# Decode block with adaLN, cached attention and a SiLU feed-forward: a smaller first transfer, and 16 value rows scaled on another engine

## The chip, the core and the metric

The kernel runs on one core of a Trainium2 chip. A core has TensorE (PE: matmuls), VectorE (DVE), ScalarE (ACT), GpSimd (POOL) and SyncE (SP), which here issues all DMAs; 16 DMA engines carry them out. The metric is the device time of one execution in microseconds (us), the median of several runs. Lower is better.

## The reference

Everything is float32. There are 4 batches, each with one token of width 512, 32 heads with 4096 cached keys and values of width 128, and a feed-forward part of width 1792.

```python
mod = (_silu(c) @ w_mod).reshape(4, 6, 1, -1)
sa, ca, ga, sb, cb, gb = (mod[:, i] for i in range(6))
h = _layernorm(x) * (1 + ca) + sa
q = (h @ wq).reshape(B, 1, H, Dh).transpose(0, 2, 1, 3)
scores = einsum("bhqd,bhkd->bhqk", q, k_cache) * Dh ** -0.5
o = einsum("bhqk,bhkd->bhqd", softmax(scores), v_cache)
x = x + ga * (o as (B, 1, H * Dh)) @ wo
h = _layernorm(x) * (1 + cb) + sb
return x + gb * (silu(h @ w1) @ w2)
```

The key and value caches are 4 x 32 x 4096 x 128 floats each, 268 MB each; they are read once. All else together is about 30 MB.

## The kernel before, in words

**Slots.** SBUF holds three slots of 64 KB per partition (`kv`, three buffers). Everything large goes through them in order: the head (`wm`: the conditioning `c`, the input `x` and the modulation weights `w_mod`), `wq`, then for each of 32 iterations n one K tile and one V tile, at the end `wo` and the two feed-forward weights. A K or V tile is 128 partitions x 128 rows x 128 floats: one batch and four heads, 32 partitions for each head. SyncE issues a transfer when its slot is free. K of the next iteration is issued at an iteration's start, V after the K reductions (`load_k`, `load_v`).

**The start.** One transfer (L118) brings the head on 128 partitions, 12320 floats each: four rows of `w_mod` per partition with 16 floats of `c` and 16 of `x` in front. Meanwhile VectorE and GpSimd build constants. When it has landed, `silu2` makes `csT`, `mods((sa, ca1), 0)` multiplies it with the weights in four steps (L200), spreads the result with a VectorE product and a small matmul for each of four groups (L208, L212; the products alternate between two halves of `mm`), then comes the layernorm, then `mods` for the other four vectors, then the query product with `wq` (L249). Small tiles of this stage lie in the head's own slot behind the weights: `mm`, `qs`, `zsel`, `csT`, `hT` and others. K1 and V0 take the slots of the head and of `wq`.

**An iteration n of the main loop.** The K tile is multiplied with the query, 104 of its 128 rows by VectorE and 24 by GpSimd (L283; the first two iterations divide it otherwise), then VectorE adds over the width (L288). Then comes a chain of small steps: row maximum (L292, VectorE), a transpose on TensorE (L296), maximum per head on VectorE (L301 to L304), exponential on ScalarE (L310), spread weights on GpSimd (L316, `pz`).

The V tile of iteration n - 1 is weighted in three ways. Rows 64 to 127 go through TensorE with the spread weights (`pv`, L356). Rows 0 to 47 are multiplied on GpSimd (L331). Rows 48 to 63 are multiplied on ScalarE, 16 activations with a scale for each partition (L330). Then GpSimd adds the 64 multiplied rows in halves, 32, 16, 8, 4 (L335), and TensorE adds the remaining four groups into the sum (`vsum`, L341), which frees V's slot. The last two V tiles go through TensorE whole.

At certain iterations finished heads are gathered and normalized (`gather`, `norm`, `spread`). After the loop come the output product, the second layernorm and the feed-forward part, whose last weights arrive in small pieces (L477 with `fetch`).

Of the kernel before, what the change touches and what calls it, by code (L numbers as in the profile page):

```python
# [9 lines left out]
F32 = mybir.dt.float32  # L10
# [7 lines left out]
def kernel(  # L18
    ctx: ExitStack,
    tc: tile.TileContext,  # L20
    head: bass.AP,
    kc: bass.AP,
    vc: bass.AP,
# [12 lines left out]
    HP = 4  # L36
# [12 lines left out]
    NK = D // P  # L49
    NI = F // P  # L50
    FG = F // G
    NA = 24
    NL = 56
    NV = 64
# [45 lines left out]
        load(vt, vc, "v", n)  # L100

    s0 = Slot("wm")
    cT, xT = s0.take(NK, B), s0.take(NK, B)
    wmt = s0.take(NK, 6 * D)
    nh = s0.at
    hg0, sa, ca1 = (s0.take(P) for _ in range(3))
    tmp = s0.take(NK, B)
    mm = s0.take(2, 4, P)
    csT, hT, xw = (s0.take(NK, W) for _ in range(3))
    CW = HP * Dh  # L110
    qs = s0.take(2, CW)
    ZB = P - NT * B // 2
    zsel = s0.take(ZB + P)

    xg = const.tile([P, P], F32, name="xg")
    nc.vector.memset(csT, 0.0)
    nc.gpsimd.memset(xw, 0.0)
    nc.sync.dma_start(s0.t[:, :nh], head)  # L118
    wqt = Slot("wq").take(NK, H * Dh)
    nc.sync.dma_start(wqt, wq.rearrange("p (k n) -> p k n", k=NK))  # L120
    load_k(0, 0, NJ // 2, NJ)
# [57 lines left out]
    nc.vector.memset(zsel, 0.0)  # L179
    nc.vector.tensor_copy(zsel[:, ZB:P].rearrange("p (g x) -> p g x", g=G), i4[:, :, ::SB])  # L180

    def silu2(dst, t, src):
        nc.scalar.activation(t, src, AF.Tanh, scale=0.5)
        nc.vector.scalar_tensor_tensor(dst, t, 1.0, src, op0=ALU.add, op1=ALU.mult)  # L184
# [10 lines left out]
    def mods(dsts, i):  # L195
        n = len(dsts)
        p = psum([P, D], "q", 2)
        for k in range(NK):
            for u in range(n):
                nc.tensor.matmul(  # L200
                    p[W * u : W * (u + 1), :], csT[:, k, :], wmt[:, k, (i + u) * D : (i + u + 1) * D],
                    start=k == 0, stop=k == NK - 1,
                )
        z = psum([P, n, P], "q", 2)
        r = W * n
        for g in range(G):
            m = mm[:r, g % 2, :n, :]
            nc.vector.tensor_mul(  # L208
                m, p[:r, g * P : (g + 1) * P].unsqueeze(1).to_broadcast([r, n, P]),
                hm[:r, :n].unsqueeze(2).to_broadcast([r, n, P]),  # L210
            )
            nc.tensor.matmul(z[W * g : W * (g + 1), :, :], sel[:r, :], m, start=True, stop=True)  # L212
        for u, d in enumerate(dsts):
            nc.scalar.activation(
                d, z[:, u, :], AF.Copy,
                scale=0.25 if i + u == 5 else 0.5, bias=1.0 if i + u in (1, 4) else 0.0,
            )
# [59 lines left out]
        qw[n] = work.tile([P, Dh], F32, tag="qw", name=f"qw{n}")  # L277
        nc.scalar.activation(qw[n], qb[n], AF.Copy)  # L278

    sc, nm, po, rs = {}, {}, {}, {}  # L280

    def mult(eng, src, n, lo, hi):
        eng.tensor_mul(  # L283
# [8 lines left out]
        nc.vector.tensor_reduce(nm[n], sc[n], axis=AX.X, op=ALU.max)  # L292

    def bmax(n):
        p = psum([P, P + HP], "mx", 2)
        nc.tensor.transpose(p[:, :P], nm[n].to_broadcast([P, P]), ident)  # L296
        nm[n] = p

    def negmax(n):
        m = nm[n][:, P:]  # L300
        nc.vector.tensor_reduce(m, nm[n][:, :P].rearrange("p (i x) -> p i x", i=HP), axis=AX.X, op=ALU.max)  # L301
# [24 lines left out]
    def vmult(n):  # L326
        if first(n):
            v = vt[n]
            for j in range(NP, NV):
                nc.scalar.activation(v[:, j, :], v[:, j, :], AF.Copy, scale=sc[n][:, j : j + 1])  # L330
            nc.gpsimd.tensor_mul(  # L331
                v[:, :NP, :], v[:, :NP, :], sc[n][:, :NP].unsqueeze(2).to_broadcast([P, NP, Dh])
            )
            for m, lo in ((32, 32), (16, 16), (8, 8), (JJ, JJ)):
                nc.gpsimd.tensor_add(v[:, :m, :], v[:, :m, :], v[:, lo : lo + m, :])  # L335
# [111 lines left out]
    for n in range(N):  # L447
        t, b = divmod(n, B)
        if n + 1 < N:
            load_k(n + 1)  # L450
        else:
            load_v(n)
        if t and b == 1:
            sums(t - 1)
        sc[n] = work.tile([P, NJ], F32, tag="sc", name=f"sc{n}")
        w, m = (NJ // 2, NL // 2) if n == 0 else (NJ, NL) if n == 1 else (NJ, NA)
        for lo in range(0, NJ, w):
            mult(nc.gpsimd, qw, n, lo, lo + m)
            mult(nc.vector, qb, n, lo + m, lo + w)
            if n + 1 < N and not lo:  # L460
                make_qb(n + 1)
            if n:
                vmult(n - 1)
                pv(n - 1)
            red(n, lo + m, lo + w)
        for lo in range(0, NJ, w):
            red(n, lo, lo + m)
        if n + 1 < N:
            load_v(n)
        else:  # L470
            so = Slot("wo")
            wat, wot = so.take(RA, D), so.take(NT - TA, R, D)
            fetch(so.t, wo, 0, RA * D, SLOT - R * D, SLOT)
            s2 = Slot("w12")
            w1t = s2.take(NK, F)
            w2t = s2.take(NI, D)
            fetch(s2.t, w12, 0, 3 * F, *(NK * F + i * D for i in (0, 5, 8, 10, 11, 12, 13, 14)))  # L477
        rowmax(n)
        bmax(n)
        if n and first(n - 1):  # L480
            vsum(n - 1)
        negmax(n)
# [69 lines left out]
def _packed(inputs):  # L552
# [39 lines left out]
```

## Time and profile before

| | before |
|---|---|
| median of 3 runs | 1319.3 us (1318.99 to 1319.37) |
| profiled execution, span from the first to the last instruction | 1317.4 us (the profile states no other time of this execution) |
| mean granted TensorE clock | 0.597 |
| VectorE busy | 1077.5 us, 82% |
| GpSimd busy | 1074.5 us, 82% |
| TensorE, ScalarE busy | 338.3 us, 196.0 us |
| DMA queue fed by SyncE | 567.31 MB, 99.5% of 16 engines' span |

How to read it: the busy share of an engine is an average over stages. The DMA share is the time in which a packet was under way, over 16 engines. In rows of instructions the columns are start, duration, engine, line, operation, output<-inputs, and in brackets the idle time before with what ended it; in grouped rows they are busy time, mean duration in ns, and idle time before with its releasers. Times are in us from the span's start.

### The profile page before, as it was taken

The numbers are of one execution on the slowest core, as the hardware profiler recorded it, in microseconds if no ns is written. First come the engines' busy times: TensorE is split into PE (matmuls) and PEld (weight loads), VectorE is DVE, ScalarE is ACT, GpSimd is POOL, SyncE is SP. The second block draws the span as 40 slices with busy tenths as digits, with TensorE's granted clock in tenths as the row PEclk, the third lists the DMA queues.
The fourth block names the chain that finished last, engine by engine and source line by source line (L and its number), as shares of the span: only waits on it lengthen the run. The fifth ranks groups of instructions, "written<-read, shape, count | busy, mean of one in ns | idle before, by whom it ended". The sixth has DMA issues, their size and how long they took to land.

```text
span 1317.4 us, 5041 instructions
## 1 busy us (share of the span) xinstructions
PE 338.3 (26%) x1636; PEld 88.8 (7%) x1636; DVE 1077.5 (82%) x357; ACT 196.0 (15%) x648; POOL 1074.5 (82%) x227
## 2 busy tenths in 40 slices
PE   3301122221212222121322122122212223221258
PEld 1100000000000000000000000000000000000013
DVE  2597888988888998888898888889888889988862
ACT  1101111110111111012111111111201121110101
POOL 0459888888988888998888899888889888889910
PEclk9756656655665565556655555655655665655569
DMA  9999999999999999999999999999999999999998
GB/s 414 436 422 444 434 428 440 424 440 440 423 440 440 426 438 434 430 437 436 432 438 428 432 440 432 432 440 430 430 442 430 432 434 436 434 434 430 440 422 342
DMA packets 11434, 567.63 MB, mean 431 GB/s; under 512 B 1280, under 2 KB 1296, under 8 KB 2192
## 3 DMA queue, kind: packets, MB, share of 16 engines
q1 hardware_dynamic: 11408, 567.31, 99.5%
q8 instruction: 13, 0.21, 0.1%
q14 instruction: 13, 0.11, 0.0%
HBM read 567.30 MB, written 0.01 MB: 431 GB/s over the span
## 4 chain that ended last, share of the span: by engine, by line
DMA 48%; DVE 28%; POOL 21%; PE 2%; issue 1%; ACT 0%; SPq 0%; DVEq 0%; POOLq 0%
DMA k<-in_A_k_cache_dram 21%; DMA v<-in_A_v_cache_dram 20%; DVE sc L288 16%; POOL v L335 13%; DVE k L283 12%; POOL v L331 8%; DMA w<-in_B_w_dram 3%; DMA wq<-in_A_wq_dram 3%; PE po L341 1%; PE q L249 1%; PE mx L259 0%; ACT qm L272 0%; PE q L274 0%; SPq L86 0%; PE od L378 0%
## 5 line engine op out<-in xcount | busy, mean ns | idle before, releaser
L283 DVE TENSOR_TENSOR k<-k,q 128x13312 f32<-128x13312 f32 (+2 forms) x33 | 440.3, 13343 | 151.2 <-DMA k<-in_A_k_cache_dram 136.4
L288 DVE TENSOR_REDUCE sc<-k 128x104 f32<-128x13312 f32 (+3 forms) x66 | 553.2, 8423 | 4.1
L335 POOL TENSOR_TENSOR v<-v 128x4096 f32<-128x4096 f32 (+1 forms) x120 | 508.9, 4241 | 9.4
L331 POOL TENSOR_TENSOR v<-v,sc 128x6144 f32<-128x6144 f32 x30 | 313.8, 10461 | 109.9 <-DMA v<-in_A_v_cache_dram 109.9
L356 PE MATMUL po<-v,pz 128*32 128x512 f32 x1088 | 193.3, 876 | 270.0 <-DMA v<-in_A_v_cache_dram 270.0
L283 POOL TENSOR_TENSOR k<-k,qw 128x3072 f32<-128x3072 f32 (+2 forms) x33 | 231.5, 7016 | 32.2 <-ACT qw L278 31.4
L341 PE MATMUL po<-v,hs 128*32 128x512 f32 x60 | 57.4, 1060 | 447.7 <-POOL v L335 447.7
L330 ACT ACTIVATE v<-v,sc 128x128 f32<-128x128 f32 x480 | 143.7, 388 | 162.8 <-DMA v<-in_A_v_cache_dram 162.8
L278 ACT ACTIVATE qw<-q 128x128 f32<-128x128 f32 x32 | 8.9, 278 | 532.8 <-DVE k L283 424.1
L356 PEld LDWEIGHTS po<-v,pz 128*32 128x32 f32 x1088 | 48.9, 153 | 417.4 <-issue 417.4
L296 PE MATMUL mx<-ident,rm 128*128 128x128 f32 x32 | 14.2, 444 | 229.6 <-DVE rm L292 229.6
L310 ACT ACTIVATE sc<-sc,nm 128x128 f32<-128x128 f32 x32 | 12.9, 402 | 328.6 <-DVE nm L304 328.6
L316 POOL TENSOR_TENSOR pz<-sc,hm 128x256 f32<-128x256 f32 x34 | 20.8, 613 | 30.6 <-ACT sc L310 30.6
L341 PEld LDWEIGHTS po<-v,hs 128*32 128x32 f32 x60 | 5.5, 140 | 456.4 <-POOL v L335 456.4
L301 DVE TENSOR_REDUCE mx<-mx 128x4 f32<-128x128 f32 x32 | 9.6, 300 | 19.4 <-PE mx L296 19.4
L296 PEld LDWEIGHTS mx<-ident,rm 128*128 128x128 f32 x32 | 5.7, 179 | 259.5 <-issue 204.9
L367 DVE TENSOR_TENSOR o<-po,jm 128x512 f32<-128x512 f32 x16 | 10.9, 681 | 12.1 <-PE po L356 12.1
L373 DVE TENSOR_REDUCE s<-o 128x128 f32<-128x512 f32 x16 | 16.6, 1036 | 0.6
L274 PE MATMUL q<-qm,blk 128*128 128x512 f32 x16 | 15.3, 1055 | 1.7 <-ACT qm L272 1.7
L200 PE MATMUL q<-wm 128*32 128x512 f32 x48 | 9.2, 681 | 18.9 <-DVE wm L184 18.9
L190 POOL COPY wm<-wm 128x16 f32<-128x16 f32 x1 | 0.2, 212 | 16.1 <-DMA wm<-in_head_dram 16.1
L272 ACT ACTIVATE qm<-qn,sel 128x128 f32<-128x128 f32 x32 | 10.2, 390 | 5.0 <-DVE oa L420 4.9
(114 smaller groups left out, 165.9 us busy)
## 6 DMA issues: line engine op xcount, KB each, us to landing
k<-in_A_k_cache_dram SPq DMA_DIRECT2D x2, 4096.0 KB, 51.8
wm<-in_head_dram SPq DMA_DIRECT2D x1, 6160.0 KB, 17.7
wo<-in_A_wo_dram SPq DMA_DIRECT2D x1, 4096.0 KB, 16.7
wo<-in_A_wo_dram SPq DMA_DIRECT2D x1, 3072.0 KB, 23.6
w<-in_B_w_dram SPq DMA_DIRECT2D x1, 2688.0 KB, 31.4
w<-in_B_w_dram SPq DMA_DIRECT2D x1, 1280.0 KB, 35.7
wo<-in_A_wo_dram SPq DMA_DIRECT2D x1, 1024.0 KB, 25.6
w<-in_B_w_dram SPq DMA_DIRECT2D x4, 256.0 KB, 17.5
```

What stands on the lines that cost most here:

```text
L249: nc.tensor.matmul(pq[i][W * g : W * (g + 1), :], hT[:, k, :], wqt[:, k, ch * CW : (ch + 1) * CW], start=k == 0, stop=k == NK - 1,)
L274: nc.tensor.matmul(p, blk.rearrange("p i x -> p (i x)"), m, start=True, stop=True)
L283: eng.tensor_mul(kt[n][:, lo:hi, :], kt[n][:, lo:hi, :], src[n].unsqueeze(1).to_broadcast([P, hi - lo, Dh]))
L288: nc.vector.tensor_reduce(sc[n][:, lo:hi], kt[n][:, lo:hi, :], axis=AX.X, op=ALU.add)
L296: nc.tensor.transpose(p[:, :P], nm[n].to_broadcast([P, P]), ident)
L316: nc.gpsimd.tensor_mul(pz[h][:, f * W : HG * W].rearrange("p (g x) -> p g x", g=m)[:, :, E:].rearrange("p g (i j) -> p g i j", i=HP), sc[n ...
L330: nc.scalar.activation(v[:, j, :], v[:, j, :], AF.Copy, scale=sc[n][:, j : j + 1])
L331: nc.gpsimd.tensor_mul(v[:, :NP, :], v[:, :NP, :], sc[n][:, :NP].unsqueeze(2).to_broadcast([P, NP, Dh]))
L335: nc.gpsimd.tensor_add(v[:, :m, :], v[:, :m, :], v[:, lo : lo + m, :])
L341: nc.tensor.matmul(po[t, q][0:W, :], hs[:, o : o + W], vt[n][:, :JJ, :].rearrange("p j d -> p (j d)"), start=False, stop=a == 1,)
L356: nc.tensor.matmul(po[t, q][W * g : W * (g + 1), :], pz[h][:, o : o + W], vt[n][:, JJ * j : JJ * (j + 1), :].rearrange("p j d -> p (j d)") ...
L373: nc.vector.tensor_reduce(s, o.rearrange("p j d -> p d j"), axis=AX.X, op=ALU.add)
```

## The change

Two things are changed.

*The head.* `w_mod` has 512 rows. The first 128 of them now come by themselves, two rows each on partitions 32 to 95 (`first_rows`). The other 384, three per partition on 128 partitions, come in a second transfer, with `c` and `x` now behind them. The modulation product thus has five steps instead of four: in the first two only 64 partitions carry weights, and the others are set to zero on VectorE and GpSimd (32 partitions each) beforehand; `c` is laid out to match. `mm` (now one buffer instead of two), `qs` and `zsel` move to memory of their own, outside of the head's slot.

*The value rows 48 to 63.* ScalarE's 16 activations are gone. ScalarE copies the 16 weights of each partition into PSUM behind the maxima (`wv`), and VectorE multiplies all 16 rows in one instruction of 128x2048 (`vrest`), in the next iteration, after its row maximum. GpSimd's adds are put in another order: rows 24 to 47 onto 0 to 23, 16 to 23 onto 0 to 7, then (`vadd`, with VectorE's result) 48 to 63 onto 0 to 15, then 8 and 4. Besides, two pieces of the last feed-forward weights come as one.

The core of the diff:

```diff
+    NH = 2
+    NM = NK - NH // 2
+    PH = slice(P // 4, 3 * P // 4)
...
+    half = wmt[:, :NH, :]
+    nc.sync.dma_start(s0.t[PH, : NH * 6 * D], first_rows)
+    nc.sync.dma_start(s0.t[:, NH * 6 * D : nh + (NH + NM + NK) * B], head)
     nc.vector.memset(csT, 0.0)
     nc.gpsimd.memset(xw, 0.0)
-    nc.sync.dma_start(s0.t[:, :nh], head)
...
+    nc.vector.memset(half[: PH.start], 0.0)
+    nc.gpsimd.memset(half[PH.stop :], 0.0)
...
-        for k in range(NK):
+        for k in range(NH + NM):
...
-            m = mm[:r, g % 2, :n, :]
+            m = mm[:r, :n, :]
...
+        if first(n):
+            nc.scalar.activation(wv[n], sc[n][:, NP:NV], AF.Copy)
...
-            for j in range(NP, NV):
-                nc.scalar.activation(v[:, j, :], v[:, j, :], AF.Copy, scale=sc[n][:, j : j + 1])
...
-            for m, lo in ((32, 32), (16, 16), (8, 8), (JJ, JJ)):
-                nc.gpsimd.tensor_add(v[:, :m, :], v[:, :m, :], v[:, lo : lo + m, :])
+            fold(n, (24, 24), (8, 16))
+
+    def fold(n, *steps):
+        v = vt[n]
+        for m, lo in steps:
+            nc.gpsimd.tensor_add(v[:, :m, :], v[:, :m, :], v[:, lo : lo + m, :])
+
+    def vadd(n):
+        if first(n):
+            fold(n, (16, NP), (8, 8), (JJ, JJ))
+
+    def vrest(n):
+        if first(n):
+            v = vt[n][:, NP:NV, :]
+            nc.vector.tensor_mul(v, v, wv[n].unsqueeze(2).to_broadcast([P, NV - NP, Dh]))
...
         rowmax(n)
+        if n:
+            vrest(n - 1)
+            vadd(n - 1)
         bmax(n)
```

How instructions move on three engines. SyncE at the program's start, before (shapes are partitions x floats):

```order
L118 DMA wm_69<-in_head_dram 128x12320
L120 DMA wq_74<-in_A_wq_dram 128x16384
L86 DMA k0_76<-in_A_k_cache_dram 128x8192 x2
L86 DMA k1_266<-in_A_k_cache_dram 128x16384
L86 DMA v0_279<-in_A_v_cache_dram 128x16384
```

And SyncE at the same place after:

```order
L122 DMA wm_69<-in_first_dram 64x6144
L123 DMA wm_69<-in_head_dram 128x9252
L127 DMA wq_78<-in_A_wq_dram 128x16384
L90 DMA k0_80<-in_A_k_cache_dram 128x8192 x2
L90 DMA k1_278<-in_A_k_cache_dram 128x16384
L90 DMA v0_291<-in_A_v_cache_dram 128x16384
```

One transfer has become two; what follows keeps its order.

VectorE at the end of iteration 3 before, from the last K reduction (`sc` are the scores, `rm` the row maximum, `mx` the PSUM tile with the transposed maxima):

```order
L288 TENSOR_REDUCE sc3_413<-k3_352 128x24
L292 TENSOR_REDUCE rm3_467<-sc3_413 128x1
L301 TENSOR_REDUCE mx_469<-mx_469 128x4
L302 TENSOR_TENSOR mx_469<-mx_469,hn_98 128x4
L304 TENSOR_REDUCE nm3_474<-mx_469 128x1
```

And VectorE at the same place after:

```order
L298 TENSOR_REDUCE sc3_400<-k3_352 128x24
L302 TENSOR_REDUCE rm3_436<-sc3_400 128x1
L359 TENSOR_TENSOR v2_380<-v2_380,mx_388 128x2048
L312 TENSOR_REDUCE mx_442<-mx_442 128x4
L313 TENSOR_TENSOR mx_442<-mx_442,hn_102 128x4
L315 TENSOR_REDUCE nm3_447<-mx_442 128x1
```

The multiply of the previous iteration's V tile has come between the row maximum and the maximum per head.

GpSimd with the V tile of iteration 1 before, up to the spread weights of iteration 2:

```order
L331 TENSOR_TENSOR v1_339<-v1_339,sc1_294 128x6144
L335 TENSOR_TENSOR v1_339<-v1_339 128x4096
L335 TENSOR_TENSOR v1_339<-v1_339 128x2048
L335 TENSOR_TENSOR v1_339<-v1_339 128x1024
L335 TENSOR_TENSOR v1_339<-v1_339 128x512
L316 TENSOR_TENSOR pz1_114<-sc2_354,hm_96 128x16x16
```

And GpSimd at the same place after:

```order
L342 TENSOR_TENSOR v1_334<-v1_334,sc1_307 128x6144
L350 TENSOR_TENSOR v1_334<-v1_334 128x3072
L350 TENSOR_TENSOR v1_334<-v1_334 128x1024
L350 TENSOR_TENSOR v1_334<-v1_334 128x2048
L350 TENSOR_TENSOR v1_334<-v1_334 128x1024
L350 TENSOR_TENSOR v1_334<-v1_334 128x512
L329 TENSOR_TENSOR pz1_118<-sc2_354,hm_100 128x16x16
```

The first add has become two smaller ones that need GpSimd's own rows alone; the add of 2048, the third now, is the first to need the rows of another engine.

More of the change, by code (lines that the diff above doesn't have):

```diff
@@ L20 @@
     tc: tile.TileContext,
+    first_rows: bass.AP,
     head: bass.AP,
@@ L102 @@
     s0 = Slot("wm")
-    cT, xT = s0.take(NK, B), s0.take(NK, B)
-    wmt = s0.take(NK, 6 * D)
+    wmt = s0.take(NH + NM, 6 * D)
     nh = s0.at
+    cT, xT = s0.take(NH + NM, B), s0.take(NK, B)
     hg0, sa, ca1 = (s0.take(P) for _ in range(3))
-    tmp = s0.take(NK, B)
-    mm = s0.take(2, 4, P)
-    csT, hT, xw = (s0.take(NK, W) for _ in range(3))
+    tmp = s0.take(NH + NM, B)
+    mm = const.tile([P, 4, P], F32, name="mm")
+    csT = s0.take(NH + NM, W)
+    hT, xw = (s0.take(NK, W) for _ in range(2))
     CW = HP * Dh
-    qs = s0.take(2, CW)
+    qs = const.tile([P, 2, CW], F32, name="qs")
     ZB = P - NT * B // 2
-    zsel = s0.take(ZB + P)
+    zsel = const.tile([P, ZB + P], F32, name="zsel")
     xg = const.tile([P, P], F32, name="xg")
+    half = wmt[:, :NH, :]
+    nc.sync.dma_start(s0.t[PH, : NH * 6 * D], first_rows)
+    nc.sync.dma_start(s0.t[:, NH * 6 * D : nh + (NH + NM + NK) * B], head)
     nc.vector.memset(csT, 0.0)
     nc.gpsimd.memset(xw, 0.0)
-    nc.sync.dma_start(s0.t[:, :nh], head)
     wqt = Slot("wq").take(NK, H * Dh)
@@ L201, in mods @@
                     p[W * u : W * (u + 1), :], csT[:, k, :], wmt[:, k, (i + u) * D : (i + u + 1) * D],
-                    start=k == 0, stop=k == NK - 1,
+                    start=k == 0, stop=k == NH + NM - 1,
                 )
@@ L278, in make_qb @@
         nc.scalar.activation(qw[n], qb[n], AF.Copy)
-    sc, nm, po, rs = {}, {}, {}, {}
+    sc, nm, po, rs, wv = {}, {}, {}, {}, {}
     def mult(eng, src, n, lo, hi):
@@ L294, in bmax @@
     def bmax(n):
-        p = psum([P, P + HP], "mx", 2)
+        p = psum([P, P + HP + NV - NP], "mx", 2)
         nc.tensor.transpose(p[:, :P], nm[n].to_broadcast([P, P]), ident)
@@ L299, in negmax @@
     def negmax(n):
-        m = nm[n][:, P:]
+        m = nm[n][:, P : P + HP]
+        wv[n] = nm[n][:, P + HP :]
         nc.vector.tensor_reduce(m, nm[n][:, :P].rearrange("p (i x) -> p i x", i=HP), axis=AX.X, op=ALU.max)
@@ L476 @@
             w2t = s2.take(NI, D)
-            fetch(s2.t, w12, 0, 3 * F, *(NK * F + i * D for i in (0, 5, 8, 10, 11, 12, 13, 14)))
+            fetch(s2.t, w12, 0, 3 * F, *(NK * F + i * D for i in (0, 5, 10, 11, 12, 13, 14)))
         rowmax(n)
+        if n:
+            vrest(n - 1)
+            vadd(n - 1)
         bmax(n)
@@ L560, in columns @@
         return a.reshape(-1, dm).T.reshape(p, -1)
+    rows, n = i["w_mod"], 2 * (p // 2)
+    c = np.zeros((p, 5, i["c"].shape[0]), i["c"].dtype)
+    c[p // 4 : 3 * p // 4, :2] = i["c"][:, :n].T.reshape(p // 2, 2, -1)
+    c[:, 2:] = i["c"][:, n:].T.reshape(p, 3, -1)
     late = i["A_wo"][half:].reshape(4, p, -1).transpose(1, 0, 2).reshape(p, -1)
     return {
-        "head": np.concatenate([columns(i["c"]), columns(i["A_x"]), i["w_mod"].reshape(p, -1)], axis=1),
+        "first": rows[:n].reshape(p // 2, -1),
+        "head": np.concatenate([rows[n:].reshape(p, -1), c.reshape(p, -1), columns(i["A_x"])], axis=1),
         "A_k_cache": i["A_k_cache"],
```

## The prediction

> **What bounds the kernel now.** I read the first page of the profile first: the engines' shares, the DMA rows, the queues.
>
> ```profile
> span 1317.4 us, 5041 instructions
> PE 338.3 (26%) x1636; PEld 88.8 (7%) x1636; DVE 1077.5 (82%) x357; ACT 196.0 (15%) x648; POOL 1074.5 (82%) x227
> DMA  9999999999999999999999999999999999999998
> DMA packets 11434, 567.63 MB, mean 431 GB/s; under 512 B 1280, under 2 KB 1296, under 8 KB 2192
> q1 hardware_dynamic: 11408, 567.31, 99.5%
> q8 instruction: 13, 0.21, 0.1%
> q14 instruction: 13, 0.11, 0.0%
> ```
>
> VectorE and GpSimd are busy for 82% each, but the queue that SyncE feeds keeps the 16 DMA engines busy for 99.5% of the span. Next the busy times by stage, from 0 to 40 us, 120 to 1040 us and the last 47 us (length, then PE, PEld, DVE, ACT, POOL busy, clock, DMA share, GB/s).
>
> ```profile
> 0.00:40.00 40.00, 16.99 (x88) 4.58 (x92) 11.27 (x47) 4.28 (x10) 2.01 (x10) 1.00 0.96 408
> 120.00:1040.00 920.00, 213.14 (x886) 50.68 (x886) 797.52 (x213) 146.84 (x497) 823.32 (x168) 0.57 1.00 434
> 1270.00:1317.40 47.40, 36.89 (x315) 13.78 (x315) 10.60 (x28) 4.67 (x9) 1.18 (x2) 0.88 0.86 363
> ```
>
> In the long middle the share is 1.00 at 434 GB/s: nothing is to be had there except by moving fewer bytes, and the change moves the same ones. What is not at that rate is the start, (434 - 408) x 40 / 434 = 2.4 us, and the end. So a faster compute engine gains nothing by itself, and a slower one costs something only if it lets the queue run dry. How far it is from that I read from the DMA issues (median us from issue to landing; KB each where all are alike).
>
> ```profile
> wm<-in_head_dram SPq DMA_DIRECT2D x1, 6160.0 KB, 17.7
> v<-in_A_v_cache_dram SPq DMA_DIRECT2D x32, 26.4
> k<-in_A_k_cache_dram SPq DMA_DIRECT2D x31, 28.1
> out_dram<-end SPq DMA_DIRECT2D x1, 8.0 KB, 1.8
> ```
>
> The head met an empty queue: 6160 KB is 6.31 MB, 14.5 us at 434 GB/s, so an idle start costs 17.7 - 14.5 = 3.2 us. One K or V transfer is 128 x 16384 x 4 B = 8.39 MB, 19.3 us. A V transfer therefore stands behind other bytes for 26.4 - 19.3 = 7.1 us, and could be issued 7.1 - 3.2 = 3.9 us later before an engine idles; a K transfer 28.1 - 19.3 - 3.2 = 5.6 us later. These two leads are the yardstick for every compute cost below.
>
> **VectorE gets 30 instructions.** The rows by form (busy, mean ns, idle before), and then VectorE in the iterations that begin near 1045 and 1084 us.
>
> ```profile
> L283 DVE TENSOR_TENSOR k<-k,q 128x13312 f32<-128x13312 f32 x30 | 420.6, 14022 | 136.4 <-DMA k<-in_A_k_cache_dram 136.4
> L367 DVE TENSOR_TENSOR o<-po,jm 128x512 f32<-128x512 f32 x16 | 10.9, 681 | 12.1 <-PE po L356 12.1
> 1044.80 14.02 DVE L283 TENSOR_TENSOR k<-k,q 128x13312 f32<-128x13312 f32 x1 [3.38 <-DMA k<-in_A_k_cache_dram]
> 1076.27 0.29 DVE L292 TENSOR_REDUCE rm<-sc 128x1 f32<-128x128 f32 x1
> 1077.18 0.30 DVE L301 TENSOR_REDUCE mx<-mx 128x4 f32<-128x128 f32 x1 [0.63 <-PE mx L296]
> 1084.12 14.02 DVE L283 TENSOR_TENSOR k<-k,q 128x13312 f32<-128x13312 f32 x1 [5.64 <-DMA k<-in_A_k_cache_dram]
> ```
>
> The new multiply of 128x2048 does not occur before. By the large product it takes 14022 x 2048 / 13312 = 2.16 us, by the small one at most 4 x 681 = 2.72 us; I take 2.2, since it is one long instruction like the first. It stands after the row maximum, where VectorE idles 0.63 us for TensorE's transpose, and that wait now runs beside it; so an iteration gains about 1.6 us of VectorE work. Behind it in the queue come the three small steps of the maximum, the exponential on ScalarE that waits for them, the gathers, and the next K product. But that product waits for K's DMA anyway: 136.4 us over 30, 4.5 us each, 3.4 us in the iteration with a gather. With 2.2 us more, and in such iterations the transpose also behind the multiply, 1.2 us of that is left. And the V transfer that follows a K reduction is released by the last reduce, ahead of the new instruction. Cost: nothing; if the cover were gone, the first 3.9 us of lateness would still lie in the lead. GpSimd's last 16-tile add now waits for this multiply. The multiply would have ended at 1076.27 + 0.29 + 2.2 = 1078.8.
>
> ```profile
> 1064.11 10.46 POOL L331 TENSOR_TENSOR v<-v,sc 128x6144 f32<-128x6144 f32 x1 [3.65 <-DMA v<-in_A_v_cache_dram]
> L335 POOL TENSOR_TENSOR v<-v 128x4096 f32<-128x4096 f32 x30 | 264.4, 8813 | 2.3
> L335 POOL TENSOR_TENSOR v<-v 128x1024 f32<-128x1024 f32 x30 | 70.6, 2354 | 2.4
> ```
>
> GpSimd reaches that add after its 10.46 us product, a 24-tile and an 8-tile add. 1024 elements cost (8813 - 2354) / 3 = 2.15 us, so 24 tiles cost 8.81 - 2.15 = 6.66 us: 1064.11 + 10.46 + 6.66 + 2.35 = 1083.6, 4.8 us after the multiply ends. No wait. The add chain is 6.66 + 2.35 instead of 8.81 ahead of the same last three adds: 0.2 us longer, plus one gap, say 0.3 us, out of a K lead of 5.6 and of 3.65 us idle. Cost: nothing. ScalarE loses 480 activations and gains 30 small ones; nobody waits for it now but the exponential.
>
> **Fewer instructions to fetch.** The two instruction queues share the DMA engines. One fetch each, from a 5 us stretch at 41 us and a 2 us stretch at 82 us (packets, MB, share of 16 engines):
>
> ```profile
> q8 instruction: 1, 0.02, 1.2%
> q14 instruction: 1, 0.01, 1.0%
> ```
>
> One 16 KB fetch holds one engine 0.012 x 16 x 5 = 0.96 us, one of 8 KB 0.010 x 16 x 2 = 0.32 us. All fetches are 0.32 MB for 5041 instructions, 63.5 B each. The 450 fewer on ScalarE are 28.6 KB, some 85 more on VectorE, GpSimd and TensorE 5.4 KB: three 8 KB fetches fewer. They help only where they sat on the engine that finishes last. The DMA row in 40 slices from 1306 to 1314 us shows that the engines don't finish together:
>
> ```profile
> DMA  9898989799899999989687867654443261210000
> ```
>
> They drop out one by one from about 1309 to 1313.4. Gain between 0 and 3 x 0.32 = 0.9 us; the larger 0.96 us fetches, which TensorE's 3272 instructions explain (0.21 MB), weigh more and stay. I take 0.1.
>
> **The start.** The bytes are the same, in 64 descriptors of 24 KB and then 128 of 37 KB instead of 128 of 49 KB. What shorter first descriptors can save is part of the 3.2 us: not more than 3.2 - 1.8 = 1.4 us, by the 16-row transfer at the end, which took 1.8 us in all; at worst nothing, since the later transfer stands in the queue before the first is done (an issue takes 0.33 us, as K3's row below shows; the first transfer's 1.57 MB take 3.6 us). I take 0.4, nearer to the old head, which it resembles more. That 64 rows still use 16 engines I read from the packets: 1280 of under 512 B are 16 for each of the 80 DMA issues, so even the 16-row output marked all 16.
>
> Here a rule speaks against the change. The Trainium skill, "SBUF — State Buffer", section "Door 1: The DMA port swizzle", says that partitions 0 to 63 reach only 8 of 16 ports and run at half rate; by its formula 32 to 95, used here, reach all 16. No trace so far shows a 64-partition load; if its half rate applied, the sum would be the rival below, if its formula does, my sum stands.
>
> The two memsets of 32x6144 are new ahead of the activations:
>
> ```profile
> 5.35 0.26 DVE L179 MEMSET wm<- 128x240 f32 x1
> 18.48 0.21 POOL L190 COPY wm<-wm 128x16 f32<-128x16 f32 x1 [16.08 <-DMA wm<-in_head_dram]
> ```
>
> At 0.26 us / 240 = 1.08 ns an element they take at most 6.7 us each, GpSimd's inside 16.08 us of waiting for the head; VectorE, idle until the same transfer lands and ScalarE's activation after it, has its own list done at 5.6 us. Nothing. (If GpSimd were twice as slow, 13.4 us would still fit.) The modulation then gets longer: five steps instead of four, and one product buffer instead of two.
>
> ```profile
> 18.94 5.52 PE L200 MATMUL q<-wm 128*32 128x512 f32 x16 [18.94 <-DVE wm L184]
> 24.51 0.75 DVE L208 TENSOR_TENSOR wm<-q,hm 64x256 f32<-64x256 f32 x2 [5.32 <-PE q L200]
> 25.63 0.75 DVE L208 TENSOR_TENSOR wm<-q,hm 64x256 f32<-64x256 f32 x2 [0.38 <-PE q L212]
> 28.17 3.64 PE L200 MATMUL q<-wm 128*32 128x512 f32 x32
> 31.88 1.29 DVE L208 TENSOR_TENSOR wm<-q,hm 128x512 f32<-128x512 f32 x2 [1.74 <-PE q L200]
> 33.77 1.29 DVE L208 TENSOR_TENSOR wm<-q,hm 128x512 f32<-128x512 f32 x2 [0.61 <-PE q L212]
> 36.20 0.79 ACT L214 ACTIVATE mod<-q 128x128 f32<-128x128 f32 x4 [7.10 <-PE q L212]
> 37.88 7.07 PE L249 MATMUL q<-wq,wm 128*32 128x512 f32 x64 [1.71 <-DMA wq<-in_A_wq_dram]
> ```
>
> A fifth step: a quarter of 5.52 and of 3.64, 1.4 + 0.9 us. One buffer: a product waits for the matmul of the one before, so each takes the distance that now holds two, 1.12 and 1.89 us: two such distances more each time, 2.2 + 3.8 us at most. That is 5 to 8.3 us on 36.99 (the last ACT row's end), against the weights that land at 37.9: the query product ends 4 to 7 us later than 44.95. I take 5.5. Behind it stand K1's load and the first products of GpSimd and VectorE, so the first transfers that feel it are V1 (issued 106.54) and K3 (127.07). The chain's V1 row, GpSimd's V0 wait, K3's issue and its landing:
>
> ```profile
> 106.54 29.23 DMA v<-in_A_v_cache_dram
> 97.31 10.46 POOL L331 TENSOR_TENSOR v<-v,sc 128x6144 f32<-128x6144 f32 x1 [1.70 <-DMA v<-in_A_v_cache_dram]
> 127.07 0.33 SPq L86 DMA_DIRECT2D k<-in_A_k_cache_dram  x1
> 155.14 14.02 DVE L283 TENSOR_TENSOR k<-k,q 128x13312 f32<-128x13312 f32 x1 [5.50 <-DMA k<-in_A_k_cache_dram]
> ```
>
> V1's lead is 29.23 - 19.3 - 3.2 = 6.7 us, K3's 28.07 - 22.5 = 5.6, of which 5.5 - 1.7 + 0.3 = 4.1 is used. Both hold, by 1.2 and 1.5 us; at the upper end V1 falls 0.3 us short. After that VectorE waits for the DMA again and the delay is gone.
>
> **The sum.** Start -0.4, fetches -0.1, the rest hidden: -0.5 us on a span of 1317.4. The median of the runs, 1319.3, lies 1.9 us above the span (the profile gives no other time of its execution); I keep that difference: 1318.8.
>
> **The rivals.** A measurement of this kernel can tell about 0.2% (2.6 us) from no change.
> - Half of the ports or engines carry the first transfer: 1.57 MB take 7.2 instead of 3.6 us, and everything behind moves by 3.6: 1322.9, slower. For it: no row times such a shape; it is what the rule quoted above would give. Against it: the 16 marks of the 16-row output. It decides as soon as fewer than about 9 of the 16 work in the first transfer. 0.06.
> - The longer modulation lets the queue run dry once at V1. It decides from 6.7 us of delay on; at 7 to 8 us it costs 0.3 to 1.3: 1319.1 to 1320.1, within 0.2%. 0.10. Past 9.3 us it would be slower (1321.9 and up), 0.02.
> - All of the bounds on the good side: 1.4 + 0.9 = 2.3 us, 1317.0, still within 0.2%. For more than 2.6 us the tail of the DMA would have to close too. Faster: 0.05.
> - The change doesn't do what it says for the time: VectorE's multiply and ScalarE's relief are both hidden and the start is as before: 1319.3. 0.15, within 0.2%.
>
> **How the numbers follow.** My forecast has the rest, 0.61. Faster 0.05; slower 0.06 + 0.02, and 0.01 for what I don't see, 0.09; same 0.86. The range goes from 1317.0 (both gains at their bounds) to 1321.0 (no gain, a dry queue of 0.8 us and one 16 KB fetch more on the last engine, 0.9), which leaves out the half-rate case and the ends.
>
> **What would show it.** Right: the middle stays at share 1.00 and 434 GB/s; the multiply takes 2.2 us; VectorE's wait for K falls to 2.3 to 3 us but not to zero; GpSimd's third add does not wait for VectorE; the first issue is followed by data earlier. Wrong: a slice below share 1.00 between 100 and 135 us (the modulation), wq landing 3 us later than before (half rate), or issue-to-landing of V falling below 22.5 us.

## The result and the profile after

The kernel after takes 1323.85 us (median of 5 runs, 1322.86 to 1324.75), before 1319.24 us (5 runs, 1318.99 to 1319.37). The ratio is 1.0035, with a 95% interval of 1.0024 to 1.0046: slower by 4.6 us, where 1318.8 and "no change" had been predicted. The profiled execution has a span of 1322.1 us against 1317.4.

First the page of the kernel after: the engines, the DMA packets, the queues.

```profile
span 1322.1 us, 4660 instructions
PE 341.2 (26%) x1648; PEld 89.3 (7%) x1648; DVE 1151.4 (87%) x388; ACT 57.7 (4%) x198; POOL 1085.5 (82%) x258
DMA packets 11367, 567.61 MB, mean 429 GB/s; under 512 B 1280, under 2 KB 1296, under 8 KB 1936
q1 hardware_dynamic: 11344, 567.31, 99.4%
q8 instruction: 13, 0.21, 0.1%
q14 instruction: 10, 0.08, 0.0%
```

The change did what it says: ScalarE is down from 196.0 to 57.7 us, VectorE up by 74 us. The queue moves the same 567.31 MB and is still busy for 99.4% of the span. But 99.4% of 1322.1 is 1314 us and 99.5% of 1317.4 was 1311: the same bytes kept the engines busy for longer. Three 8 KB instruction fetches are gone, as predicted, with nothing to show for it.

Next the compute rows that the prediction put at nothing, from the groups by form (busy, mean ns, idle time before).

```profile
L293 DVE TENSOR_TENSOR k<-k,q 128x13312 f32<-128x13312 f32 x30 | 420.6, 14021 | 83.2 <-DMA k<-in_A_k_cache_dram 83.2
L359 DVE TENSOR_TENSOR v<-v,mx 128x2048 f32<-128x2048 f32 x30 | 68.3, 2277 | 0.0
L350 POOL TENSOR_TENSOR v<-v 128x2048 f32<-128x2048 f32 x30 | 135.8, 4527 | 2.4
```

The new multiply takes 2.28 us (2.2 predicted). VectorE's wait for K falls from 136.4 to 83.2 us, 2.8 us an iteration, and is still there: the multiply lies inside it. GpSimd's add of 2048, which needs VectorE's result, idles 2.4 us in 30 times, 0.08 us each: it does not wait.

The DMA issues (KB, median us from issue to landing):

```profile
wm<-in_first_dram SPq DMA_DIRECT2D x1, 1536.0 KB, 6.7
wm<-in_head_dram SPq DMA_DIRECT2D x1, 4626.0 KB, 17.0
v<-in_A_v_cache_dram SPq DMA_DIRECT2D x32, 26.5
k<-in_A_k_cache_dram SPq DMA_DIRECT2D x31, 28.0
```

The first transfer on 64 partitions ran at full rate: 1.57 MB are 3.6 us at 434 GB/s, and with the 3.2 us of an idle start that makes 6.8, against 6.7 measured (at half rate it would be 10.4). The formula in the Trainium skill, "SBUF — State Buffer", section "Door 1: The DMA port swizzle", by which partitions 32 to 95 reach all ports, agrees with that. The head is complete 17.0 us after an issue at 1.44 us, at 18.4 us; before, it was 0.74 + 17.7 = 18.4. The start gained nothing. SyncE's first row after:

```profile
0.74 0.64 SPq L122 DMA_DIRECT2D wm<-in_first_dram  x1
```

And before:

```profile
0.74 0.39 SPq L118 DMA_DIRECT2D wm<-in_head_dram  x1
```

The issue on partitions 32 to 95 takes 0.25 us longer, and in the trace's packet records the first packet starts at 2.17 us, where it was 1.76 before. What follows in the queue is behind by 0.4 to 0.5 us.

So where are 4.6 us? The stages of the kernel after, with the stage 40:120 of the kernel before behind them (columns as in the prediction: length, PE, PEld, DVE, ACT, POOL, clock, DMA share, GB/s).

```profile
0.00:40.00 40.00, 17.53 (x73) 4.76 (x74) 18.74 (x44) 3.49 (x6) 7.22 (x11) 0.91 0.96 407
40.00:120.00 80.00, 20.68 (x124) 6.42 (x122) 63.13 (x23) 7.01 (x21) 47.29 (x6) 0.68 1.00 426
120.00:1040.00 920.00, 209.85 (x885) 50.09 (x885) 844.95 (x230) 35.60 (x134) 831.23 (x193) 0.57 1.00 433
```

The same view of the kernel before:

```profile
40.00:120.00 80.00, 14.43 (x100) 5.45 (x92) 59.63 (x18) 10.65 (x31) 53.96 (x7) 0.61 1.01 438
```

Two places differ. From 40 to 120 us the rate is 426 instead of 438 GB/s: 80 x 12 / 434 = 2.2 us. And the long middle has 433 instead of 434, with a share of 1.00 all the same. That last digit would be worth 920 / 434 = 2.1 us if it is real, and it is at the edge of what the view can say. I therefore follow the starts of VectorE's big K product, first in the iterations at 155 and 1239 us (the kernel after; before, the first began at 155.14).

```profile
156.59 14.02 DVE L293 TENSOR_TENSOR k<-k,q 128x13312 f32<-128x13312 f32 x1 [4.52 <-DMA k<-in_A_k_cache_dram]
1242.84 14.02 DVE L293 TENSOR_TENSOR k<-k,q 128x13312 f32<-128x13312 f32 x1 [4.55 <-DMA k<-in_A_k_cache_dram]
```

The kernel before in the later of them:

```profile
1238.55 14.02 DVE L283 TENSOR_TENSOR k<-k,q 128x13312 f32<-128x13312 f32 x1 [4.87 <-DMA k<-in_A_k_cache_dram]
```

After is late by 1.45 us at 155, 2.3 us an iteration later, and 4.3 us at 1239. Both kernels wait for the DMA at each of these rows. There is a step at the start and then a drift: the 28 iterations take 1242.84 - 156.59 = 1086.25 us, against 1238.55 - 155.14 = 1083.41, 0.10 us more each.

The step begins in the modulation. TensorE's two modulation products (the second, for four vectors, with 40 matmuls), the small matmul behind each group, ScalarE's end of the stage and K1's issue, in the kernel after:

```profile
19.01 6.76 PE L210 MATMUL q<-wm 128*32 128x512 f32 x20 [19.01 <-DVE wm L194]
26.29 0.62 PE L222 MATMUL q<-mm,sel 64*32 64x256 f32 x2 [0.51 <-DVE mm L218]
27.41 0.62 PE L222 MATMUL q<-mm,sel 64*32 64x256 f32 x2 [0.51 <-DVE mm L218]
31.61 7.30 PE L210 MATMUL q<-wm 128*32 128x512 f32 x40
39.82 1.02 PE L222 MATMUL q<-mm,sel 128*32 128x512 f32 x2 [0.92 <-DVE mm L218]
46.36 0.78 ACT L224 ACTIVATE mod<-q 128x128 f32<-128x128 f32 x4 [14.03 <-PE q L222]
53.59 0.33 SPq L90 DMA_DIRECT2D k<-in_A_k_cache_dram  x1
```

The second product takes 7.30 us where five quarters of 3.64 are 4.55. The granted clock says why (same view by stage; the clock is the third number from the end):

```profile
24.00:30.50 6.50, 4.46 (x20) 1.10 (x15) 2.05 (x6) 0.18 (x2) 0.00 (x0) 1.00 1.12 484
30.50:37.30 6.80, 6.30 (x31) 1.88 (x35) 1.56 (x6) 1.81 (x4) 0.00 (x0) 0.50 0.88 381
```

For 6.8 us TensorE ran at half its clock; before, it was granted the full clock for all of the first 40 us. The Trainium skill, "TensorE: Matmul & The Clock Gate", section "What's actually happening", has the clock fall to half after an idle window of about 3.4 us, and these windows run on their own time; 6.8 us is two of them. The trace agrees with the length but not with the condition: in the stretch ahead of the fall, from 24.0 to 30.5 us, TensorE was busy for 4.46 of 6.5 us and no gap was longer than 0.52 us. K1 was issued at 53.59 us, against 45.00 before, and V1 at 114.53 against 106.54: 8.6 and 8.0 us late.

VectorE in the next K stage of the kernel after:

```profile
114.54 0.28 DVE L302 TENSOR_REDUCE rm<-sc 128x1 f32<-128x128 f32 x1
114.74 2.28 DVE L359 TENSOR_TENSOR v<-v,mx 128x2048 f32<-128x2048 f32 x1
117.55 14.02 DVE L293 TENSOR_TENSOR k<-k,q 128x13312 f32<-128x13312 f32 x1
```

The K product at 117.55 doesn't wait: here alone the multiply of 2.28 us lies on the way. It costs next to nothing, since this K tile, issued at 85.95 us, landed 31.5 us later, only 0.1 us ahead of the product. K1 and V1 are the two late issues that can have left a hole in the queue before 120 us; how much each of them did is taken up at the end of the experiments.

### The profile page after: what moved, and what is told of

The parts are those of the page before. It is cut to its first block, busy times and chain, and to the rows that moved or that the text cites. A ratio compares the mean times of both kernels' runs of the same rounds, so it can differ in the third digit from the quotient of the medians.

```text
span 1322.1 us, 4660 instructions
## 1 busy us (share of the span) xinstructions
PE 341.2 (26%) x1648; PEld 89.3 (7%) x1648; DVE 1151.4 (87%) x388; ACT 57.7 (4%) x198; POOL 1085.5 (82%) x258
## 3 DMA queue, kind: packets, MB, share of 16 engines
q1 hardware_dynamic: 11344, 567.31, 99.4%
## 4 chain that ended last, share of the span: by engine, by line
DMA 44%; DVE 31%; POOL 20%; PE 4%; issue 1%; ACT 0%; SPq 0%; DVEq 0%; POOLq 0%
DMA k<-in_A_k_cache_dram 21%; DMA v<-in_A_v_cache_dram 18%; DVE sc L298 17%; DVE k L293 13%; POOL v L350 13%; POOL v L342 7%; DMA wo<-in_A_wo_dram 2%; PE po L365 1%; DMA w<-in_B_w_dram 1%; DMA wm<-in_head_dram 1%; PE q L210 1%; PE q L259 1%; PE q L222 0%; DVE v L359 0%; DVE mm L218 0%
## 5 line engine op out<-in xcount | busy, mean ns | idle before, releaser
L350 POOL TENSOR_TENSOR v<-v 128x1024 f32<-128x1024 f32 (+3 forms) x150 | 515.0, 3433 | 11.8
L293 DVE TENSOR_TENSOR k<-k,q 128x13312 f32<-128x13312 f32 (+2 forms) x33 | 440.3, 13342 | 96.0 <-DMA k<-in_A_k_cache_dram 83.2
L380 PE MATMUL po<-v,pz 128*32 128x512 f32 x1088 | 189.6, 862 | 252.4 <-DMA v<-in_A_v_cache_dram 252.4
L359 DVE TENSOR_TENSOR v<-v,mx 128x2048 f32<-128x2048 f32 x30 | 68.3, 2277 | 0.0
L218 DVE TENSOR_TENSOR mm<-q,hm 64x256 f32<-64x256 f32 (+1 forms) x8 | 4.4, 554 | 17.8 <-PE q L210 12.2
L210 PE MATMUL q<-wm 128*32 128x512 f32 x60 | 14.1, 883 | 19.0 <-DVE wm L194 19.0
L526 PE MATMUL q<-mod,ident 128*128 128x512 f32 (+2 forms) x24 | 10.7, 555 | 0.0
```

Source lines behind the costliest of these rows:

```text
L210: nc.tensor.matmul(p[W * u : W * (u + 1), :], csT[:, k, :], wmt[:, k, (i + u) * D : (i + u + 1) * D], start=k == 0, stop=k == NH + NM - 1,)
L293: eng.tensor_mul(kt[n][:, lo:hi, :], kt[n][:, lo:hi, :], src[n].unsqueeze(1).to_broadcast([P, hi - lo, Dh]))
L359: nc.vector.tensor_mul(v, v, wv[n].unsqueeze(2).to_broadcast([P, NV - NP, Dh]))
L380: nc.tensor.matmul(po[t, q][W * g : W * (g + 1), :], pz[h][:, o : o + W], vt[n][:, JJ * j : JJ * (j + 1), :].rearrange("p j d -> p (j d)") ...
```

## The experiments

**First theory**, formed on these rows: the late modulation is the only cause; the queue runs dry once and the loop keeps the lateness. Rivals: the multiply on VectorE costs something after all; the two transfers, or the new layout of the head in DRAM, cost something.

**The two halves of the change apart.** `v_only` is the kernel before with the value rows on VectorE alone:

```diff
-            for j in range(NP, NV):
-                nc.scalar.activation(v[:, j, :], v[:, j, :], AF.Copy, scale=sc[n][:, j : j + 1])
...
+            nc.vector.tensor_mul(v, v, wv[n].unsqueeze(2).to_broadcast([P, NV - NP, Dh]))
```

> The kernel before with the value part alone: VectorE scales the 16 rows, the head comes as before. Dry-queue theory (the longer modulation holds back K1 and V1 until the DMA engines idle): K1 issued near 45 us as before, 1319.3, ratio within 0.1% of 1. Loop theory (the new multiply slows the steady loop): at least 2 us slower, 1321.3 or more, with the middle stage below 434 GB/s.

Measured: 1319.47 us, ratio 1.0003 [0.9993, 1.0012]. `head_only` is the kernel before with the head's part alone (and the two pieces of the last weights as one):

```diff
+    nc.sync.dma_start(s0.t[PH, : NH * 6 * D], first_rows)
+    nc.sync.dma_start(s0.t[:, NH * 6 * D : nh + (NH + NM + NK) * B], head)
...
+    mm = const.tile([P, 4, P], F32, name="mm")
+    qs = const.tile([P, 2, CW], F32, name="qs")
+    zsel = const.tile([P, ZB + P], F32, name="zsel")
```

> The changed kernel with ScalarE's 16 activations and GpSimd's adds as before; only the head differs from the kernel before. Dry-queue theory: K1 issued near 53.6 us, 1322 to 1324, nearly the whole loss. Loop theory: under 1321.

Measured: 1323.82 us, ratio 1.0036 [1.0022, 1.005]. The whole loss is in the head's part. The groups of `v_only` by form show why the other half is free:

```profile
L283 DVE TENSOR_TENSOR k<-k,q 128x13312 f32<-128x13312 f32 x30 | 420.6, 14021 | 86.9 <-DMA k<-in_A_k_cache_dram 86.9
L349 DVE TENSOR_TENSOR v<-v,mx 128x2048 f32<-128x2048 f32 x30 | 68.3, 2277 | 0.0
```

VectorE's wait for K shrinks from 136.4 to 86.9 us, 49.5 us, and the span (1317.6) does not move.

**One z buffer, and a late K1, in the kernel before.** `mm1` takes one product buffer instead of two:

```diff
-            m = mm[:r, g % 2, :n, :]
+            m = mm[:r, 0, :n, :]
```

> The kernel before with one product buffer in the modulation instead of two, nothing else. Dry-queue theory: the granted clock falls in the modulation, the query product ends 6 to 8 us later than at 45.0, part of the loss appears: 1320.5 to 1323. Loop theory, or a theory that blames the two transfers: no change, 1319.3.

Measured: 1321.14 us (1319.39 to 1321.97), ratio 1.0014 [1.0005, 1.0023]; in its profiled execution, at a span of 1317.6, K1 was issued at 50.07 us, 5.1 us late (6 to 8 were expected), and the K product at 155 began at 155.19: that execution, the fastest of the ten, lost nothing, while the ten runs are spread over 2.6 us. So the edge is near. `late_k1` delays the query product by 11 matmuls whose result is not used, and leaves all else as before:

```diff
+    late = psum([P, D], "po", 2)
+    for _ in range(11):
+        nc.tensor.matmul(late, ident, mod.rearrange("p a x -> p (a x)"), start=True, stop=True)
```

> The kernel before with 11 matmuls into an unused tile ahead of the query product, nothing else; one transfer for the head. It is a delay alone. Dry-queue theory: K1 issued near 53.5 us and the whole loss, 1322 to 1324.5, with the slow drift over the loop if that is a consequence of the dry queue. Rival (two transfers or places in memory): no more than the late start itself, under 1321.5 and no drift.

Measured: 1323.26 us (1321.59 to 1325.15), ratio 1.0029 [1.0019, 1.0038]; K1 at 54.87, 9.9 us late. Its K products in the two iterations:

```profile
158.94 14.02 DVE L286 TENSOR_TENSOR k<-k,q 128x13312 f32<-128x13312 f32 x1 [8.07 <-DMA k<-in_A_k_cache_dram]
1242.51 14.02 DVE L286 TENSOR_TENSOR k<-k,q 128x13312 f32<-128x13312 f32 x1 [4.86 <-DMA k<-in_A_k_cache_dram]
```

3.80 us late at 155 and 3.96 at 1239: a step as the theory wants it, kept to the end, and no drift. A late start alone thus makes the kernel slower, but not in the way of the kernel after.

**The second buffer back.** A second product buffer of its own (`mm2`) does not fit into SBUF: the pool behind it needs 5.09 KB per partition and 4.28 KB are left, so there is no time for it. `two_buf` is the kernel after with half of `qs`, not yet in use then, as a second product buffer:

```diff
+    mq = qs[:, 1, :].rearrange("p (a x) -> p a x", a=4)
...
-            m = mm[:r, :n, :]
+            m = (mm, mq)[g % 2][:r, :n, :]
```

> The changed kernel with two product buffers in the modulation again; the second one borrows the half of qs that is written only later. Dry-queue theory: TensorE pauses less and keeps its clock, K1 is issued at 47 to 49 us instead of 53.6 and the time is 1319 to 1320.5. Rival (two transfers or the other places in memory cost by themselves): no change from the changed kernel, 1323 to 1324.

Measured: 1322.58 us, ratio 1.0024 [1.0014, 1.0034]. K1 is issued at 46.31, only 1.3 us late, and the step is gone:

```profile
155.00 14.02 DVE L294 TENSOR_TENSOR k<-k,q 128x13312 f32<-128x13312 f32 x1 [4.17 <-DMA k<-in_A_k_cache_dram]
1241.62 14.02 DVE L294 TENSOR_TENSOR k<-k,q 128x13312 f32<-128x13312 f32 x1 [4.54 <-DMA k<-in_A_k_cache_dram]
```

But at 1239 it is 3.1 us late, and the time is far from the 1319 to 1320.5 us expected. The first theory falls: most of the loss here came without a late start.

**The transfers and their place in DRAM.** `split128` is the kernel before with the head in two transfers, both on 128 partitions (one row of `w_mod` each, then three); `pad2k` is the kernel before with 16 bytes more per partition in the head, 2 KB in all, which shifts what lies behind it in DRAM if the tensors lie there one behind the other (not shown).

```diff
+    nc.sync.dma_start(wmt[:, 0, :], first_rows)
+    nc.sync.dma_start(s0.t[:, 6 * D : nh], head)
```

> The kernel before with its head in two transfers, both on 128 partitions: one weight row each, then three rows with c and x; four modulation steps as before. Dry-queue theory: K1 issued within 1 us of 45.0, 1319 to 1320. Rival (two transfers cost by themselves, through the longer first issues or the other places in memory): 1322 or more, K products drifting apart from those of before by about 2 us over the loop.

> The kernel before with four floats of padding per partition in the head, 2 KB in all, which is by how much the changed head is larger; it moves the caches in memory by as much if tensors lie one behind the other. Dry-queue theory: 1319.3, no change. Rival (places in memory): 1320.5 or more with K products drifting apart over the loop.

Measured: 1319.22 us, ratio 0.9999 [0.9989, 1.0008], and 1319.24 us, ratio 1.0 [0.9991, 1.001]. Neither costs anything.

**Second theory.** What is left of the head's part is memory: `mm`, `qs` and `zsel` moved out of the head's slot to a place ahead of the three slots. They hold 512, 1024 and 240 floats per partition, 7104 bytes. Before, the slots began at byte 19200 of each partition, which is 75 x 256; now they begin at 26304 = 102 x 256 + 192. Every large transfer then writes rows that don't start on a multiple of 256 bytes. Here a rule of the Trainium skill bears on it: "DMA: Bandwidth & Descriptors", section "How a descriptor splits into AXI transactions", says that a descriptor (here one row) is cut into pieces of 256 bytes that start on multiples of 256, and that a start in between is fetched from the multiple below it, with bytes that are not used. It speaks of reading; that it holds for writing into SBUF is an assumption. By its count a 64 KB row would be 257 pieces instead of 256; an estimate from that, 1083 / 256, is 4.2 us for the loop. The rival was that something else in the head's part causes the drift.

**The slots shifted in the kernel before.** `before_192` and `before_64` put one unused tile of 192 or 64 bytes ahead of the slots (and fill it with zeros at the start). In `before_192`:

```diff
+    gap = const.tile([P, 48], F32, name="gap")
+    nc.vector.memset(gap, 0.0)
```

> The kernel before with one unused tile of 192 bytes ahead of the slots, so that they begin at byte 19392 (192 beyond a multiple of 256) instead of 19200 (a multiple). Nothing else is changed but a small memset of that tile. Theory of the place of the slots: a drift of 2 to 3.5 us over the loop with K1 issued at 45.0 us as before, so 1321.3 to 1322.8 us. Rival, that the place does nothing: 1319.0 to 1319.5 us.

> As the last one with an unused tile of 64 bytes, so that the slots begin at byte 19264 (64 beyond a multiple of 256). If any place off a multiple of 256 bytes costs the same, the drift and the time are those of the run with 192 bytes, 1321.3 to 1322.8 us; if only some places cost, 1319.0 to 1319.5 us.

Measured: 1322.24 us (1321.96 to 1322.55), ratio 1.0023 [1.0014, 1.0033], and 1322.3 us (1322.04 to 1322.42), ratio 1.0023 [1.0013, 1.0033]. K1 is issued at 44.95 and 44.75, as before. The K products of `before_192`:

```profile
155.01 14.02 DVE L285 TENSOR_TENSOR k<-k,q 128x13312 f32<-128x13312 f32 x1 [5.60 <-DMA k<-in_A_k_cache_dram]
1240.90 14.02 DVE L285 TENSOR_TENSOR k<-k,q 128x13312 f32<-128x13312 f32 x1 [4.96 <-DMA k<-in_A_k_cache_dram]
```

No step, and 2.35 us late at 1239. An unused tile of 64 bytes costs 3 us, as much as one of 192.

**The kernel after with the slots on a multiple.** `after_al` has the gap of 64 bytes, so that the slots begin at 26368 = 103 x 256; `two_buf_al` has the gap and the second buffer.

```diff
+    gap = const.tile([P, 16], F32, name="gap")
+    nc.vector.memset(gap, 0.0)
```

> The kernel after, with an unused 64-byte tile behind the single buffers, so that the three K and V slots begin at byte 26368 of each partition (a multiple of 256) instead of 26304 (192 beyond a multiple of 256). The modulation still has one buffer for z. Theory of two causes (a queue that runs dry at the start, and a drift of the loop from the place of the slots): the step at the start stays (K1 issued near 53.6 us, the second K product and those after it 1.5 to 2.3 us late by 200 us), the drift is gone (no more than 2.5 us late at the last K product), so 1321.0 to 1321.7 us. Rival, one cause (the late start alone, which the loop never makes up and which makes it slower): unchanged, 1323.5 to 1324.5 us.

> The kernel after with the second z product buffer and with the slots at byte 26368. Theory of two causes: both are gone, so 1319.0 to 1319.5 us, K1 issued near 46.3 us and no K product over 0.5 us late. Rival, that the place of the slots does nothing and something else in the moved tiles or the shorter head causes the drift: 1322.3 to 1322.9 us, as with the second buffer alone.

Measured: `after_al` 1321.63 us, ratio 1.0029 [1.0008, 1.0049] (the medians give 1.0018; the ratio and its wide interval take in one of the ten runs that took 1335.25), `two_buf_al` 1319.61 us, ratio 1.0003 [0.9994, 1.0012]. The K products of `after_al`:

```profile
156.77 14.02 DVE L295 TENSOR_TENSOR k<-k,q 128x13312 f32<-128x13312 f32 x1 [5.50 <-DMA k<-in_A_k_cache_dram]
1240.07 14.02 DVE L295 TENSOR_TENSOR k<-k,q 128x13312 f32<-128x13312 f32 x1 [4.51 <-DMA k<-in_A_k_cache_dram]
```

1.63 us late at 155, 1.52 at 1239: the step alone. With both mended, 0.4 us is left, which the measurement can't tell from nothing.

The 28 iterations between the two rows, in all 14 profiled executions, worked out as above:

| where the slots begin | kernels | us for 28 iterations |
|---|---|---|
| a multiple of 256 | before, `v_only`, `mm1`, `late_k1`, `split128`, `pad2k`, `after_al`, `two_buf_al`, `after_warm` | 1083.1 to 1084.4 |
| 192 beyond | after, `head_only`, `two_buf`, `before_192` | 1085.7 to 1086.6 |
| 64 beyond | `before_64` | 1086.2 |

These figures hang on the latest part of a transfer, since a K product starts only when all of its tile is there. The traces hold 16 landing records for each transfer, and their mean is steadier. From K3's transfer to that of 28 iterations later it moves by 1082.9 to 1083.3 us in the nine kernels of the first line, by 1085.0 to 1085.1 in the four of the second and by 1085.05 in `before_64`: 2 us more, the same for both offsets. The rest of the 3 us by which `before_192` and `before_64` are slower as a whole lies outside of these iterations or with the latest records, and was not followed.

**The clock.** `after_warm` is `after_al` with ten small matmuls, whose results are not used, in TensorE's gaps of the first modulation product and the layernorm:

```diff
+            nc.tensor.matmul(warm[:, :P], ident, ident, start=True, stop=True)
...
             nc.tensor.matmul(z[W * g : W * (g + 1), :, :], sel[:r, :], m, start=True, stop=True)
+            if n == 2:
+                fill(2)
...
-    layernorm_mod(hg0, xg, sa, ca1)
+    layernorm_mod(hg0, xg, sa, ca1, lambda: fill(2))
```

> The kernel after with the slots at byte 26368 (no drift), and with ten small matmuls of 128x128 that nobody reads put into TensorE's gaps of the first modulation product and its layernorm, two behind each group's matmul. Theory that TensorE's granted clock falls to half because the chain with a single z buffer leaves TensorE idle between groups: the clock stays at 1.00 from 30 to 38 us, the second modulation product takes 4.5 to 4.6 us (5/4 of 3.64) instead of 5.9 to 7.3, K1 is issued at 50.3 to 51.8 us, and the time is 1319.3 to 1321.2 us. Rival, that the clock falls for another reason (at fixed times, or by what the product itself draws): 5.9 to 7.3 us again, K1 at 52.8 us or later, 1321.0 to 1322.0 us.

Measured: 1319.91 us, ratio 1.0005 [0.9995, 1.0014]. Its second modulation product:

```profile
32.41 4.50 PE L218 MATMUL q<-wm 128*32 128x512 f32 x40
```

And the stage around it:

```profile
30.00:37.00 7.00, 6.91 (x57) 2.92 (x55) 2.09 (x10) 1.99 (x4) 0.00 (x0) 1.00 0.88 379
```

The full clock and 4.50 us, five quarters of 3.64, as the theory asked. K1 came at 51.59, 6.6 us late, and the K product at 155 at 156.22, 1.1 us late. Without the fillers the second product was slowed in each of the six kernels with one buffer or five steps (5.00 to 7.30 us). But it was slowed in `v_only` too (5.34 instead of 3.64, with two buffers and four steps), and not in the six other kernels of that form, before among them. All ten runs of `after_warm` (1319.40 to 1320.51) lie below the fastest of `after_al` (1321.00), so what the fillers gain is not the chance of one execution, and they speak for idle time on TensorE as the cause. The single buffer is not needed for it: `two_buf` and `two_buf_al` have two, and their second product took 6.17 and 6.20 us. When exactly the clock falls stays open.

**Where the queue ran dry.** The middle of a transfer's 16 landing records shows it, in pairs of kernels with their slots at the same place. In the kernel after, against `two_buf`, it is 0.8 us later for K1, V0 and K2, 1.8 for V1 and 2.0 from K3 on: the queue lost 0.8 us at K1, 1.0 at V1 and 0.2 at K3. In `after_al`, against `two_buf_al`, it lost nothing at K1 and 1.2 us at V1; in `after_warm` nothing at K1, 0.1 at V1 and 1.1 at K3; in `late_k1`, against the kernel before, 0.9 at K1 and 3.3 at V1.

The same records show why the lead is shorter than reckoned. In the kernel before, the 16 of K2, the transfer ahead of V1, lie between 114.0 and 116.5 us. The lead of 6.7 us counts from the last of them; from the first it is 114.0 - 106.54 - 3.2 = 4.3 us, and the edge that the runs show, 5 to 6 us, lies between the two. That the engines done first then stand idle is how I read this; the records don't name the engine.

## Why the prediction was wrong

- **Right: the loop's compute.** The multiply took 2.28 us, lies in VectorE's wait for K, and `v_only` measures it at nothing. GpSimd's reordered adds don't wait for it. Half of the ports was rightly held unlikely: 6.7 us for the first transfer.
- **Wrong by its size: the fifth step, at half the clock.** The prediction added "a quarter of 5.52 and of 3.64, 1.4 + 0.9 us" for the step and 2.2 + 3.8 us at most for the one buffer. In the kernel after, the first product grew by 1.2 us (in the kernels with four steps it varies from 4.98 to 6.49) and the second by 3.7, and the stretches with the one buffer by 2.1 and 3.1. So one term failed, the 0.9: it took the full clock for granted, and the second product ran at half of it. The stage ended 10.2 us later (47.14 against 36.99), and K1 was 8.6 us late, outside of the 4 to 7 given, where 5.5 was taken. At the full clock it would have been 8.6 - (7.30 - 4.55) = 5.8 us, an estimate, and it was 6.6 in `after_warm`, whose second product began 0.8 us later than that of the kernel after; both lie inside the 4 to 7. What makes the clock fall is likely, not shown (see above).
- **Wrong by its size: V1's lead.** It was put at 6.7 us, and K1, itself the first late transfer, was given none. In `mm1`, `after_warm`, `after_al` and `late_k1`, all with the slots on a multiple, V1 was late by 5.1, 6.0, 7.2 and 9.8 us, and the K product at 155 by 0.05, 1.1, 1.6 and 3.8. The lateness beyond some 5 to 6 us is passed on. The rival that the longer modulation lets the queue run dry once at V1 was the right mechanism, with too late a start and too low a chance, and the hole was at K1 and K3 as well. Nor is the delay gone once VectorE waits for the DMA again, as the prediction has it: `late_k1` is 3.80 us late at 155 and 3.96 at 1239. Worth: 2.0 us (`after_al` against `two_buf_al`).
- **Missing: the place of the slots.** That `mm`, `qs` and `zsel` "move to memory of their own" was costed at nothing by not being costed. It moved the slots by 7104 bytes, off a multiple of 256, and the loop, whose pace is that of the K and V transfers, became about 0.2% longer. Worth: 3.0 us (`before_192` against before; `two_buf` against `two_buf_al`), 2.2 by the kernel after against `after_al`.
- **The wrong way: the start's gain of 0.4 us.** The first packet came 0.4 us later, not earlier. By the middle of the landing records the second half of K0 is there at 56.74 us in `two_buf_al`, at 56.27 before and at 56.26 in `split128`, whose two transfers are on 128 partitions. That fits the 0.4 us by which `two_buf_al` is slower than before, which the run times alone can't tell from nothing. The fetches (0.1) can't be seen.

2.0 + 3.0 + 0.4 is 5.4 us, against 4.6 measured for all together; the 0.8 between lies within the intervals of these runs (some 1.5 us to either side for after alone). Of what would show it wrong, the prediction named a share below 1.00 between 100 and 135 us. That sign can't tell: the share of this stretch is 0.98 before and 0.99 after. The other one, V from issue to landing in less than 22.5 us, was nearly there and is hidden in a median over 32 transfers: V1 took 22.6 us, where it had taken 29.2 before.

## What to carry to other kernels

In this kernel, bound by its DMA queue, the share of busy engines did not show the loss. Following one row per iteration (its start, before and after) did, and a step and a drift fell apart at once. When a change allocates or frees anything in SBUF, see where the large tiles behind it begin, modulo 256 bytes. Count the lead of a transfer from the first landing of the transfer ahead, not from the last. And where a chain of small matmuls with gaps stands ahead of a long product on TensorE, cost the product at half the clock as well: here it was slowed in seven of the thirteen kernels without fillers.

## What the runs showed of the hardware

- A destination 64 or 192 bytes beyond a multiple of 256 made transfers of 64 KB rows slower by about 0.2%, the same for both: 2 us in 1083 us of loop by the means of the landing records, 2.5 and 2.8 us by the K products of `before_192` and `before_64`. The estimate from the Trainium skill's rule above, 4.2 us, has the sign right and is 1.5 to 2.1 times too high.
- A halved TensorE clock followed a stretch in which TensorE was busy for 4.46 of 6.5 us, and ten matmuls of about 0.35 us that filled the gaps kept it at 1.00 in the execution profiled.
- A transfer on partitions 32 to 95 alone landed 6.7 us after its issue on an idle queue, 1536 KB, where 6.8 are reckoned at the full rate. Its issue took 0.64 us instead of 0.39.
- The 16 landing records of one queued transfer of 64 KB rows lie up to 2.5 us apart (K2 before: 114.0 to 116.5 us).
